# A gated mix of cached attention and an MLP on one core: the first load of wq as two transfers, 16 rows and 112 rows, and the second load of wq issued behind the end of the tile context

## The chip, the core and the metric

The kernel runs on one core of one Trainium2 chip. The metric is the device time of one execution in microseconds. Of the kernel before there are three runs: 773.12, 773.18 and 773.3 us, a median of 773.18 us. All times inside an execution come from one execution that the hardware profiler recorded, and are counted from the first instruction.

## What is computed

The reference is one decoding step for two sequences, in float32:

```python
def _A_ref(x, k_cache, v_cache, wq, wo):        # x: 2 x 1 x 1024
    q = (x @ wq)                                # 32 heads of 128
    scores = q . k_cache * Dh ** -0.5           # 4 key heads, 32768 cached positions
    o = softmax(scores) . v_cache
    return o @ wo
def _B_ref(x, w1, w2, w3, w4):
    x1 = x + hs                                 # hs: a shift by one or two positions
    return x1 + gelu(layernorm(x1) @ w3) @ w4
g = sigmoid((x * gate_w).sum(-1))
out = g * _A_ref(...) + (1 - g) * _B_ref(...)
```

With one position per sequence the shifted part `hs` is zero, so w1 and w2 are never read. What has to be read is wq (16.8 MB), w3 (14.7 MB), the caches of keys and values (268 MB together), w4 (14.7 MB) and wo (16.8 MB): 331 MB for a result of 8 KB.

## The kernel before, in words

All large arrays pass through two buffers in SBUF, `ring[0]` and `ring[1]`, each 128 rows (partitions) of 65,536 bytes. The host has laid out wq, w3, the caches, w4 and wo so that a load is 128 rows of one run of bytes each; a load of wq is a full buffer, 8 MB, and wq is two loads.

The order of the loads is written out by hand for SP (SyncE), which issues them all on its queue: wq (two loads), w3 (two), then for each of eight turns two loads of keys and two of values, w4 between the fourth and the fifth turn, and wo at the end. A load into a buffer is issued when the work on that buffer's former content is done: `load` (line 217) lets SP wait for a mark of another engine and then issues the transfer, which adds 16 to a semaphore `landed[j]` when it has landed. The engine that uses the buffer waits for that 16 and takes it off again (`take`, line 51).

The two loads of wq are the exception. They wait for nothing and are issued at line 245, inside the tile context, before it is closed (`tc.close()`, line 248, and `tc.compile()`, line 249). At the closing all engines drain their queues and meet at semaphores. Everything else in the kernel stands behind it: ScalarE issues the small load of x and the gate's weights (`xg`, line 278), GpSimd and VectorE clear buffers, and SP goes on to the loads of w3, of which the first waits for the mark `q0`.

The prologue on TensorE begins with three small products for the layernorm's sums and the padded copy of x (lines 342 to 348). Then `project` (line 361) multiplies x by wq: for each of the two loads it takes 16 off `landed[T]`, runs 64 matmuls over that buffer and sets a mark, `q0` after the first and `q1` after the second. The same function is called again for w3, with the marks `h0` and `h1`.

The rows and the engines that move them matter here: `run(wq, j)` (line 221) is the view of load j as 128 rows, and `flat[j]` (line 224) is the buffer as 128 rows. The output store at the end (line 640) takes 8 rows of a small buffer, rows 28 to 35, of 1 KB each.

Of the kernel before, what the change touches and what calls it, by code (L numbers as in the profile page):

```python
# [14 lines left out]
P = 128  # L15
B, D, HQ, HKV, SK, DH, F = 2, 1024, 32, 4, 32768, 128, 3584
# [12 lines left out]
CHUNK = D // G // 2  # L29
ROWS = G * B // 2  # L30
BASE = C - ROWS


class Line:
# [39 lines left out]
def kernel(  # L74
# [52 lines left out]
    nc = tc.nc  # L127
    scale = DH ** -0.5

    def new(name, *shape, parts=P):  # L130
        return nc.alloc_sbuf_tensor(name, [parts, *shape], F32).ap()

    def bank(name):
        return nc.alloc_psum_tensor(name, [P, 512], F32).ap()
# [6 lines left out]
    x_pad = new("x_pad", KD, C)  # L141
# [6 lines left out]
    o_last = o_wide[:, :, C - B:]  # L148
    spread = new("spread", BASE + ROWS + C)
    w_pad = new("w_pad", KF, C)  # L150
# [33 lines left out]
    sc = [bank(f"sc{i}") for i in range(NI)]  # L184
# [10 lines left out]
    def sem(name):  # L195
        cleared.append(nc.alloc_semaphore(name))
        return cleared[-1]

    stored = nc.alloc_semaphore("stored")
    pe, dve, act, pool = (Line(e, sem(n)) for e, n in (  # L200
        (nc.tensor, "pe"), (nc.vector, "dve"), (nc.scalar, "act"), (nc.gpsimd, "pool")))
    sp = Line(nc.sync)

    landed = [sem(f"landed{i}") for i in range(2)]
# [3 lines left out]
    copied = sem("copied")  # L208
    middle = slice(BASE, BASE + 2 * ROWS)

# [6 lines left out]
    def load(dst, src, sem, *marks):  # L217
        sp.after(*marks)
        nc.sync.dma_start(dst, src).then_inc(sem, 16)

    def run(src, j):
        return src[PART * j:PART * (j + 1)].rearrange("i (q w) c -> (i q) (w c)", w=PART)

    flat = [t.rearrange("p w c -> p (w c)") for t in ring]
# [7 lines left out]
    def at(name, m=None):  # L232
        if m is None:
            return (pe.sem, 1 + PROLOGUE.index(name))
        return (pe.sem, len(PROLOGUE) + m * len(TURN) + m // 4 * 2 + 1 + TURN.index(name))
# [6 lines left out]

    early = [nc.sync.dma_start(flat[j], run(wq, j)).then_inc(landed[j], 16) for j in range(2)]
    for inst in early:
        tc.no_tile_sem_insts.add(inst.ins.name)
    tc.close()
    tc.compile()

    load(flat[0][:, :PART * 2 * F], run(w3, 0), landed[0], at("q0"))
    load(flat[1][:, :PART * 2 * F], run(w3, 1), landed[1], at("q1"))

# [59 lines left out]
    dve.after(at("run"), zeroed)  # L313
    nc.vector.tensor_copy(spread[:, BASE:][:, :2 * ROWS], compact)
    for i in range(2):
        own = slice(i * HALF, (i + 1) * HALF)
# [34 lines left out]
    def columns(t, pad, k, kk, n, banks):  # L351
        quarter = n // G
        for c, b in enumerate(banks):
            lo, hi = c * 512, min(c * 512 + 512, quarter)
            for g in range(G):
                o = kk * n + g * quarter
                last = nc.tensor.matmul(b[C * g:C * g + C, :hi - lo], pad[:, k], t[:, o + lo:o + hi],  # L357
                                        start=(k == 0), stop=(k == KD - 1))
        return last

    def project(pad, n, banks):
        for T in range(4 // PART):
            pe.take(landed[T], 16)
            for kk in range(2 * PART):
                last = columns(flat[T], pad, 2 * PART * T + kk, kk, n, banks)
            done = pe.mark(last)
        return done
# [16 lines left out]
    def block(c, *quarters, **flags):  # L384

        def lhsT(half, quarter):
            return o_wide[:, c, C - B - (1 - half) * BASE - quarter % 2 * B:][:, :C]

# [8 lines left out]
                          lambda which, t: so_far[:, t * CHUNK:(t + 1) * CHUNK], (0, None), (1, None))  # L397

    pe.after(d_x)
    done = project(x_pad, HQ * DH, sc[0:2])  # L400
    dve.after(done)
    d_q = dve.mark(nc.vector.tensor_copy(row[:, 0], sc[0]))
    act.after(done)
# [14 lines left out]
    done = pe.mark(last)  # L418
    dve.after(done)
    for i in range(2):  # L420
        own = slice(i * HALF, (i + 1) * HALF)
# [9 lines left out]
    for k2 in range(2):  # L431
        for g in range(G):
            lo = P * (1 - k2)
            nc.tensor.matmul(acc[C * g:C * g + C], xr_pad[:, 2 * g + k2], wide[:, lo:lo + 2 * P],
                             start=(k2 == 0), stop=False, skip_group_check=True)
    done = project(xn_pad, F, sc[2:4])
    dve.after(done)
    d_h = dve.mark(nc.vector.tensor_copy(row[:, 0], sc[2]))
    act.after(done)
    a_h = act.mark(nc.scalar.copy(row[:, 1, :F // G - 512], sc[3][:, :F // G - 512]))  # L440
    n = KF // G
# [13 lines left out]
    done = pe.mark(last)  # L455
# [10 lines left out]
    for i in range(2):  # L466
        for j in range(2):
            own = slice(i * HALF, (i + 1) * HALF)
# [139 lines left out]
    for t, apart, lo, n in ((w_pad, C // B, 0, half), (o_last, 1, half, 2)):  # L608
        for i in range(2):
            own = slice(i * HALF, (i + 1) * HALF)  # L610
# [65 lines left out]
```

## Time and profile before

| What | Value |
|---|---|
| median of three runs | 773.18 us (773.12 to 773.3) |
| span of the profiled execution, first to last instruction | 771.6 us; a time of its own is not given beside it |
| median less span | 1.6 us |
| TensorE's matmuls busy | 436.4 us, 57% of the span |
| packets of SP's queue, as a share of 16 DMA engines | 99.4% |
| read from memory | 331.36 MB, 429 GB/s over the span |
| SP's issue of the two loads of wq | from 0.73 us, 0.87 us together |
| issue of xg, from ScalarE | 2.39 us |
| first matmul on wq | 28.38 us |
| issue of the first load of w3 | 38.09 us |

A busy share of an engine is an average over the whole span. The row of the DMA engines says how much of the time the 16 engines hold a packet; a packet here is mostly one row of a load, 65,536 bytes. A stretch of time in a view counts a packet where it starts, so a short stretch can show more than 100%.

### The profile page before, as it was taken

The page shows a single profiled execution, that of the slowest core. Times are in us where ns is not written, and L with a number is a line of the kernel's source. Part 1 is how long each engine was busy: PE and PEld are TensorE (multiplying, and loading weights), DVE is VectorE, ACT ScalarE, POOL GpSimd, SP SyncE. Part 2 cuts the span into 40 slices and gives each one's busy share as a digit, 9 for nine tenths or more (in the row PEclk, how much of TensorE's full clock was granted, in tenths as well). Part 3 has the DMA queues.
Part 4 walks back from the last instruction along what each step waited for, and adds up shares of the span by engine and source line. Part 5 has one row for each costly group of instructions (what it writes and reads, how often), then busy time and mean ns, then how long its engine had stood idle before and what let it go on. Part 6 is the DMA issues. An engine that isn't in the chain of part 4 may idle for free. (4 is left out here: it accounts for less than half of the span.)

```text
span 771.6 us, 7439 instructions
## 1 busy us (share of the span) xinstructions
PE 436.4 (57%) x3332; PEld 199.9 (26%) x3332; DVE 95.2 (12%) x269; ACT 60.7 (8%) x144; POOL 3.8 (0%) x13
## 2 busy tenths in 40 slices
PE   0676746564645474546575446454745565646467
PEld 0232413232322232223233213121322232313134
DVE  1110202100210021002100002100210021002110
ACT  0000002000200020002000002000200020002000
POOL 1000000000000000000000000000000000000000
PEclk9977667767787768767766678777777677678788
DMA  9999999999999999999999999999999999999997
GB/s 381 435 436 436 435 436 435 436 436 431 428 431 431 435 435 435 435 435 435 430 428 440 432 435 435 435 435 435 435 435 435 431 431 435 431 435 431 431 424 327
DMA packets 6648, 331.50 MB, mean 430 GB/s; under 512 B 872, under 2 KB 1008, under 8 KB 1264
## 3 DMA queue, kind: packets, MB, share of 16 engines
q1 hardware_dynamic: 6496, 331.36, 99.4%
q8 instruction: 7, 0.11, 0.1%
q10 hardware_dynamic: 144, 0.01, 0.0%
q14 instruction: 1, 0.01, 0.0%
HBM read 331.36 MB, written 0.01 MB: 429 GB/s over the span
## 5 line engine op out<-in xcount | busy, mean ns | idle before, releaser
L488 PE MATMUL sc<-load,q_cur 128*32 128x512 f32 x1024 | 144.1, 722 | 132.3 <-PEq L53 132.3
L514 PE MATMUL pv<-load,pt 128*32 128x512 f32 x1024 | 134.2, 683 | 88.7 <-PEq L53 88.7
L488 PEld LDWEIGHTS sc<-load,q_cur 128*32 128x32 f32 x1024 | 51.2, 130 | 219.2 <-issue 214.8
L514 PEld LDWEIGHTS pv<-load,pt 128*32 128x32 f32 x1024 | 39.2, 124 | 173.9 <-issue 173.9
L505 PE MATMUL sc<-wide,p 128*128 128x128 f32 x256 | 44.5, 347 | 22.8 <-PEq L53 22.8
L571 DVE TENSOR_REDUCE mx<-sc 128x1 f32<-128x512 f32 x32 | 21.4, 689 | 284.8 <-PE sc L488 284.8
L555 ACT ACT_TABLE_LOAD x8 | 10.3, 1283 | 483.0 <-ACTq L53 483.0
L505 PEld LDWEIGHTS sc<-wide,p 128*128 128x128 f32 x256 | 40.1, 184 | 30.0 <-issue 30.0
L371 PE MATMUL acc<-load,w_pad 128*32 128x256 f32 x448 | 34.2, 478 | 18.9 <-PEq L53 18.9
L588 DVE COPY pt<-sc 64x256 f32<-64x256 f32 x64 | 25.9, 414 | 81.4 <-PE sc L505 80.9
L561 ACT COPY pt<-sc 64x256 f32<-64x256 f32 x64 | 23.5, 368 | 85.3 <-PE sc L505 83.0
L593 DVE COPY pv_sb<-pv 128x512 f32<-128x512 f32 x16 | 10.3, 686 | 145.6 <-PE tr L520 145.6
L371 PEld LDWEIGHTS acc<-load,w_pad 128*32 128x32 f32 x448 | 18.6, 137 | 33.6 <-issue 28.7
L524 PE MATMUL tr<-sel,pv_sb 128*128 128x8 f32 x128 | 18.9, 284 | 11.8 <-PEq L53 11.8
L555 ACT ACTIVATE p<-sc,bias 128x512 f32<-128x512 f32 x32 | 21.6, 686 | 0.1
L357 PE MATMUL sc<-load,x_pad 128*32 128x512 f32 x128 | 19.2, 768 | 4.1 <-PEq L53 4.1
L524 PEld LDWEIGHTS tr<-sel,pv_sb 128*128 128x128 f32 x128 | 18.4, 228 | 12.3 <-issue 12.3
L357 PE MATMUL sc<-load,xn_pad 128*32 128x384 f32 (+1 forms) x128 | 15.3, 641 | 7.9 <-PEq L53 7.9
L342 PE MATMUL tr<-xg_sb,perm 128*128 128x16 f32 x4 | 1.0, 372 | 25.2 <-DMA xg_sb<-xg 25.2
L584 DVE COPY p<-p 128x256 f32<-128x256 f32 x32 | 9.4, 294 | 26.7 <-ACT p L555 26.7
L357 PEld LDWEIGHTS sc<-load,xn_pad 128*32 128x32 f32 x128 | 4.8, 130 | 18.4 <-issue 18.4
L357 PEld LDWEIGHTS sc<-load,x_pad 128*32 128x32 f32 x128 | 4.9, 137 | 17.6 <-issue 17.5
(89 smaller groups left out, 96.3 us busy)
## 6 DMA issues: line engine op xcount, KB each, us to landing
load<-w SPq DMA_DIRECT2D x4, 7168.0 KB, 24.9
load<-wo SPq DMA_DIRECT2D x1, 7168.0 KB, 29.0
load<-wo SPq DMA_DIRECT2D x1, 4608.0 KB, 19.3
load<-wo SPq DMA_DIRECT2D x1, 2560.0 KB, 25.0
tail<-wo SPq DMA_DIRECT2D x1, 1024.0 KB, 27.0
tail<-wo SPq DMA_DIRECT2D x1, 640.0 KB, 28.1
load<-kt SPq DMA_DIRECT2D x16, 29.6
load<-vt SPq DMA_DIRECT2D x16, 29.5
```

What stands on the lines that cost most here:

```text
L357: last = nc.tensor.matmul(b[C * g:C * g + C, :hi - lo], pad[:, k], t[:, o + lo:o + hi], start=(k == 0), stop=(k == KD - 1))
L371: inst = nc.tensor.matmul(acc[C * g:C * g + C], lhsT, rows[:, g * (D // G):(g + 1) * (D // G)], start=False, stop=last, skip_group_check=True)
L488: last = nc.tensor.matmul(sc[i][C * g:C * g + C], q_cur[:, w, s], ring[j][:, w, o:o + 512], start=(s == 0 and w == 0), stop=(s == 1 and w ...
L505: last = nc.tensor.transpose(sc[k][:, t * P:(t + 1) * P], pair.rearrange("p w q -> p (w q)"), ident)
L514: last = nc.tensor.matmul(pv[C * g:C * g + C], pt[j][w][:, lo:lo + C], ring[j][:, w, o:o + G * DH], start=(j == 0 and w == 0 and t == 0), ...
L524: last = nc.tensor.matmul(tr[1][:, w * REP:(w + 1) * REP], pv_sb[:, s, w].rearrange("p i q -> p (i q)"), sel[:, s], start=(s == 0), stop=( ...
L555: nc.scalar.activation(p[:, i, :, :PART], sc[i].rearrange("p (t q w) -> p t w q", t=NT, w=PART), AF.Exp, bias=bias, scale=scale, accum_out ...
L561: nc.scalar.copy(*halves(1, j, c)).then_inc(pt_in, 1)
L571: last = [nc.vector.reduce_max(out=mx[:, k:k + 1], in_=sc[k], axis=AX.X) for k in ((1, 2) if i == 2 else (i,))][-1]
L584: nc.vector.tensor_copy(p[:, i, :, PART], p[:, i, :, 0]).then_inc(to_pe, 1)
L588: nc.vector.tensor_copy(*halves(0, j, c)).then_inc(pt_in, 1)
L593: last = nc.vector.tensor_copy(pv_sb[:, :, :, i], pv.rearrange("p (s q w) -> p s w q", q=HALF, w=PART))
```

## The change

The first load of wq is cut in two at row 16. Both pieces are issued before the tile context is closed, one behind the other, and each adds 16 to the first load's semaphore when it has landed, which therefore comes to 32. `project` takes as many sixteens off the semaphore as there were transfers: two for the first half of wq, one elsewhere. The second load of wq moves from line 245 to the first place behind the closing and is issued by `load` without a mark to wait for.

```diff
+FIRST = 16
...
-    early = [nc.sync.dma_start(flat[j], run(wq, j)).then_inc(landed[j], 16) for j in range(2)]
+    early = [nc.sync.dma_start(flat[0][own], run(wq, 0)[own]).then_inc(landed[0], 16)
+             for own in (slice(0, FIRST), slice(FIRST, P))]
     for inst in early:
         tc.no_tile_sem_insts.add(inst.ins.name)
     tc.close()
     tc.compile()
 
+    load(flat[1], run(wq, 1), landed[1])
     load(flat[0][:, :PART * 2 * F], run(w3, 0), landed[0], at("q0"))
     load(flat[1][:, :PART * 2 * F], run(w3, 1), landed[1], at("q1"))
...
-    def project(pad, n, banks):
+    def project(pad, n, banks, loads=(1, 1)):
         for T in range(4 // PART):
-            pe.take(landed[T], 16)
+            pe.take(landed[T], 16 * loads[T])
...
-    done = project(x_pad, HQ * DH, sc[0:2])
+    done = project(x_pad, HQ * DH, sc[0:2], (2, 1))
```

## The prediction

> **What bounds the kernel now.** I read the page's own summary first: span, activity in 40 slices, and the DMA queues.
>
> ```profile
> span 771.6 us, 7439 instructions
> PE 436.4 (57%) x3332; PEld 199.9 (26%) x3332; DVE 95.2 (12%) x269; ACT 60.7 (8%) x144; POOL 3.8 (0%) x13
> ...
> DMA  9999999999999999999999999999999999999997
> GB/s 381 435 436 436 435 436 435 436 436 431 428 431 431 435 435 435 435 435 435 430 428 440 432 435 435 435 435 435 435 435 435 431 431 435 431 435 431 431 424 327
> ...
> q1 hardware_dynamic: 6496, 331.36, 99.4%
> ...
> PE 1%; DVE 0%; issue 0%
> ```
>
> The 16 DMA engines hold packets of SP's queue (q1) for 99.4% of the span, at a flat 435 GB/s. PE is busy 57%. The flow dips only in the first slice and the last. So the kernel is one long transfer of 331 MB, and time that an engine loses anywhere in it is hardly made up: the 0.6% in which q1 is not busy is 4.6 us, and most of it is the head and the tail. The chain of waits that ended last covers 1% of the span, its end, so it says nothing of the start, where the change lies. I went on to the DMA view of single stretches: the last line before "issues" is a queue's packets, MB and the time of its packets as a share of 16 engines in that stretch.
>
> The first packets (0 to 3 us), then the second ones (4 to 6 us):
>
> ```profile
> q1 hardware_dynamic: 16, 1.05, 106.3%
> ```
>
> ```profile
> q1 hardware_dynamic: 16, 1.05, 121.0%
> ```
>
> In each stretch 16 packets start, of 1.05 MB together, so each is one row of 65,536 bytes and each engine starts one. The second ones take 1.21 x 2 us x 16 / 16 = 2.42 us, which is 65,536 B / 2.42 us = 27.1 GB/s per engine, and 16 x 27.1 = 433 GB/s, the flat rate above. The first ones take 1.063 x 3 us = 3.19 us. I call 2.42 us a **slot**: a load of wq is 128 rows, 8 slots of each engine, 19.3 us.
>
> Then the start, from the timeline, and the finely cut table by stretches (second column: length; the last two: DMA share and GB/s), which has the first packet of wq, and below it the first packet of the output store:
>
> ```profile
> 0.73 0.87 SPq L245 DMA_DIRECT2D load<-wq  x2
> 2.39 0.42 POOL L279 MEMSET wide<- 128x384 f32 x1 [1.95 <-POOLq L249]
> 2.39 0.37 ACTq L278 DMA_DIRECT2D xg_sb<-xg  x1
> ...
> 25.10 0.17 DVE L309 TENSOR_TENSOR xw<-xg_sb 128x16 f32<-128x16 f32 x1 [18.75 <-DMA xg_sb<-xg]
> ...
> 28.38 1.94 PE L357 MATMUL sc<-load,x_pad 128*32 128x512 f32 x8
> ```
>
> ```profile
> 1.70:1.75 0.05, 0.00 (x0) 0.00 (x0) 0.00 (x0) 0.00 (x0) 0.00 (x0) 1.00 0.00 0
> 1.75:1.80 0.05, 0.00 (x0) 0.00 (x0) 0.00 (x0) 0.00 (x0) 0.00 (x0) 1.00 20.15 6554
> ```
>
> ```profile
> 38.09 0.33 SPq L219 DMA_DIRECT2D load<-w  x1
> ```
>
> ```profile
> 770.23 0.37 SPq L640 DMA_DIRECT2D out<-out_sb  x1
> ```
>
> ```profile
> 770.90:771.00 0.10, 0.00 (x0) 0.00 (x0) 0.00 (x0) 0.00 (x0) 0.00 (x0) 1.00 0.00 0
> 771.00:771.05 0.05, 0.00 (x0) 0.00 (x0) 0.00 (x0) 0.00 (x0) 0.00 (x0) 1.00 0.24 61
> ```
>
> SP issues both loads of wq from 0.73 to 1.60, and the closing of the tile context (L249) lets the engines go at 2.39. The DMA flows from 1.75 on. The first w3 load is issued at 38.09, when PE has done with the first half of wq; by the slots, both wq loads are through at 1.77 + 0.77 (the first packets' excess) + 16 x 2.42 = 41.3. Issue to first packet is 1.0 us, so some 2 us of cover remain there.
>
> **The change, part by part.**
>
> *Two issues for the first load.* SP still issues two transfers ahead of the closing (16 and 112 rows, where it was 128 and 128), at about 0.4 us each, so xg and the memsets still start at 2.39. The store has 8 rows and goes from issue 770.23 to packet about 771.02, 0.8 us; wq has 128 rows and goes from 0.73 to about 1.77, 1.04 us. If the rows make the difference, 16 rows start up to 0.24 us sooner; if not, 0. I take -0.2, as 16 is nearer to 8 rows.
>
> *The second piece* is issued 0.4 us behind the first, so its packets are due at about 2.2, while the first packets last until 1.77 + 3.19 = 4.96. No gap; were that cover gone, it would cost the 0.4 us of one issue.
>
> *The second load of wq behind the closing.* Its issue goes from 1.2 to 2.39, past the drains and semaphores of the closing in SP's queue. Its packets are needed when the first load ends, at about 21.9 us. Cover: 18 us; cost 0. Behind it on SP stands only the first w3 load, which waits for PE until 38.09 anyway.
>
> *PE's wait for 32 instead of 16* on the first landing is one instruction as before: 0. First wq lands at 21.9, PE starts on it at 28.38 (it waits for x), so 6.5 us of delay of this load alone are hidden from PE, but not from the DMA engines themselves.
>
> *Which rows are in flight together.* This is the part that decides, and no transfer of before shows it: every large one spans all 128 rows. The nearest is the output store, of 8 neighbouring rows (28 to 35); its packets, from 770.9 to 771.3 us:
>
> ```profile
> DMA packets 16, 0.01 MB, mean 21 GB/s; under 512 B 8, under 2 KB 16, under 8 KB 16
> ...
> q1 hardware_dynamic: 16, 0.01, 8.0%
> ```
>
> Eight data packets and eight small completions: eight rows went to eight engines, a row each. So 16 rows will go to 16 engines, rows 0 to 15 all at once. Before, each engine had eight of the 128 rows. Now suppose that the way into SBUF, and not the engine, is what carries 27.1 GB/s, and that a way serves eight fixed rows (128 / 16). Then 16 neighbouring rows use fewer than 16 ways. If neighbours lie on different ways, the cost is 1 slot, as now; if a way has eight adjacent rows, only 2 ways are used and the piece takes 8 slots. I take **4 slots** (four ways), the power of two just above the middle (2.8) of 1 and 8. The store speaks mildly against: 8.0% x 0.4 us x 16 = 0.51 us for 8 packets and 8 completions, at most 64 ns per KB, where a fourfold shared way would give 1,024 B / 27.1 GB/s x 4 = 151 ns. But its packets are too short to be surely in flight together, and they read SBUF, where the load writes it.
>
> For the 112 rows the same supposition works on seven consecutive rows per engine (112 / 16). Where nobody shares it is 7 slots, where each engine shares with one other all the time it is 14. I take **11**, the middle rounded up, as sevens don't fall on the borders of sets of eight.
>
> [...]
>
> *Sum.* The first load takes 4 + 11 = 15 slots of the slowest engine instead of 8: 7 x 2.42 = **+16.9 us**. It isn't made up, since every later load gives each engine its eight rows. x comes late too: its packets wait behind rows (2.39 to 25.10, 9 slots), so it comes about 7 slots later, at 42; PE is done with the first half of wq at 38.1 + 16.9 = 55.0, and the wq loads end at 41.3 + 16.9 = 58.2. The cover of 2 us there stays. Base: the profiled execution has a span of 771.6; its own time is not given beside it, so I take the median of the runs, 773.18, 1.6 above the span, and leave that distance as it is. 773.2 - 0.2 + 16.9 = **789.9 us**.
>
> **Rivals.**
>
> *No sharing* (the engine, not the way, is the limit): 1 + 7 slots as before, and only the earlier start is left: 773.2 - 0.2 = 773.0, between 772.9 and 773.2. For it: the store's short packets, and a rate that is as flat as an engine's own limit would make it. Against it: nothing in the trace singles out the engine. This is the case on the other side: not slower, and it decides as soon as a way carries four rows at full rate, 4 x 27.1 = 108 GB/s.
>
> *Only the first piece collides*: 4 slots, then 7 without sharing, or 8 if the ways that stood idle meanwhile still have eight rows to take. +3 to +4 slots: 7.3 to 9.7 us less 0.2, 780.3 to 782.7. For it: the 112 rows may be dealt to engines as the 128 are, which run clean.
>
> *The 112 rows are dealt out by every 16th*: row 16 to the first engine, 17 to the second. Then each of the seven rounds is like the first piece, 8 x 4 = 32 slots instead of 8, +58 us, 831. For it: the store gave neighbours to different engines; against it, that also fits blocks, as a block there was one row.
>
> *The pieces leave a gap*, so that the split does not do what it says: at most one issue and its latency, 0.4 + 1.0 us, if the second piece were generated only after the first is through; 774.4. The 128-row loads already follow one another without a gap, so I count it in with no sharing.
>
> **How the numbers follow.** The forecast with sharing in both pieces 0.48, only the first piece 0.18, every 16th 0.08, no sharing with or without a gap 0.26. Sharing in one form or another has 0.74: its loss is 7 to 58 us, and I have no form of it below 0.2% (1.55 us, about what a measurement of this kernel can tell from no change). Faster by over 0.2% would take 1.55 us at the head, where 0.24 is to be had: 0.01; the rest of no sharing, 0.25, is within. The forecast's own range is 785 to 797: 9 to 14 slots in the place of 11, which is 5 to 10 slots lost. The range for 8 in 10 runs from no sharing, 772.8, to 795; it leaves out every 16th and the far end of the forecast.
>
> **What would show it.** Right: 16 first packets of some 9.7 us instead of 3.19 in the first microseconds, packets of the next rows that take 2.4 to 5 us, DMA rates of 100 to 350 GB/s up to some 38 us and 435 after, x at about 42, the first w3 issue at about 55. Wrong: second packets of 2.42 us that start at 5 us and x still at 25; then the sum is the head alone. If the first packets take 9.7 and the following 2.42, the 11 was wrong; if the w3 issue comes after the wq loads have ended, a gap joins the sum that I have put at nothing.

## The result, and the profile after

The changed kernel takes **794.8 us** (median of five runs, 793.67 to 795.82), the kernel before 773.18 us beside it (773.11 to 773.3). The ratio is 1.0278, with a 95% interval of 1.0265 to 1.029: slower by 21.6 us. The profiled execution of the changed kernel took 794.8 us itself, with a span of 793.3 us, 1.5 us less; in the kernel before the distance was 1.6 us, so all of the difference lies inside the span.

The changed kernel's page, its summary, the DMA row and the rate in 40 slices (one slice is 19.8 us):

```profile
span 793.3 us, 7440 instructions
PE 433.2 (55%) x3332; PEld 199.2 (25%) x3332; DVE 95.1 (12%) x269; ACT 60.6 (8%) x144; POOL 3.8 (0%) x13
...
DMA  9999999999999999999999999999999999999997
GB/s 159 265 413 418 429 426 427 453 430 424 426 439 446 430 426 426 439 446 430 426 433 426 448 430 426 433 436 443 430 426 433 436 443 426 430 433 426 440 422 315
...
q1 hardware_dynamic: 6512, 331.36, 99.3%
```

The engines look as busy as before, 99.3% against 99.4%, and the same 331.36 MB go through. Only the rate tells: 159 and 265 GB/s in the first two slices, where it was 381 and 435, somewhat less than before in the third and fourth, and the old rate behind. The loss of the first two slices against before is (381 - 159 + 435 - 265) / 435 x 19.8 = 18 us. So a packet that crawls counts as busy, and the busy share of the DMA engines says nothing of their speed; the GB/s beside it does. The 16 more packets (888 under 512 B against 872) are the completions of the one transfer more.

The start of the changed kernel, from the timeline and from the table by stretches (last two columns: DMA share and GB/s):

```profile
0.73 0.85 SPq L246 DMA_DIRECT2D load<-wq  x2
2.36 0.35 SPq L220 DMA_DIRECT2D load<-wq  x1
2.37 0.42 POOL L282 MEMSET wide<- 128x384 f32 x1 [1.93 <-POOLq L251]
2.37 0.38 ACTq L281 DMA_DIRECT2D xg_sb<-xg  x1
...
46.98 0.18 DVE L312 TENSOR_TENSOR xw<-xg_sb 128x16 f32<-128x16 f32 x1 [40.65 <-DMA xg_sb<-xg]
...
59.30 0.35 SPq L220 DMA_DIRECT2D load<-w  x1
```

```profile
1.70:1.75 0.05, 0.00 (x0) 0.00 (x0) 0.00 (x0) 0.00 (x0) 0.00 (x0) 1.00 0.00 0
1.75:1.80 0.05, 0.00 (x0) 0.00 (x0) 0.00 (x0) 0.00 (x0) 0.00 (x0) 1.00 52.39 6554
...
12.00:22.00 10.00, 0.00 (x0) 0.00 (x0) 0.00 (x0) 0.00 (x0) 0.00 (x0) 1.00 0.80 210
22.00:32.00 10.00, 0.00 (x0) 0.00 (x0) 0.00 (x0) 0.00 (x0) 0.00 (x0) 1.00 0.93 230
32.00:42.00 10.00, 0.00 (x0) 0.00 (x0) 0.00 (x0) 0.00 (x0) 0.00 (x0) 1.00 1.09 276
42.00:52.00 10.00, 3.67 (x20) 2.28 (x24) 2.30 (x15) 1.42 (x2) 0.00 (x0) 1.00 0.93 400
```

The closing ends at 2.37 as before (2.39), and the first packet starts between 1.75 and 1.80 as before: nothing starts sooner. From 12 to 42 us the DMA moves 210 to 276 GB/s, about half of the 435 of before. x, whose small packets go between the rows (the first starts at 15.54 us, before at 7.34), comes at 46.98 instead of 25.10, 21.9 us later; PE's first mark and with it the first w3 load come 21.2 us later.

The first packets, those that start between 0 and 3 us, in the DMA view of the changed kernel:

```profile
q1 hardware_dynamic: 16, 1.05, 288.0%
```

They last 2.88 x 3 us = 8.64 us on average; before it was 3.19. Last, the loads of wq issued ahead of the closing, from issue to landing (shortest, median, longest), in the kernel before and in the changed one:

```profile
DMA to landing us min/median/max: 21.9/31.4/40.8
```

```profile
DMA to landing us min/median/max: 12.3/27.8/43.4
```

The first load of wq was issued at 0.73 and landed at 22.6. Now its 112 rows, issued at 1.2, land at 44.6: 22.0 us later. That is the whole difference of the kernel (21.6 us), and it is all in one load of 8 MB.

### The profile page after: what moved, and what is told of

It reads as the page before. It is cut to its first block, busy times and chain, and to the rows that moved or that the text cites. A ratio compares the mean times of both kernels' runs of the same rounds, so it can differ in the third digit from the quotient of the medians.

```text
span 793.3 us, 7440 instructions
## 1 busy us (share of the span) xinstructions
PE 433.2 (55%) x3332; PEld 199.2 (25%) x3332; DVE 95.1 (12%) x269; ACT 60.6 (8%) x144; POOL 3.8 (0%) x13
## 3 DMA queue, kind: packets, MB, share of 16 engines
q1 hardware_dynamic: 6512, 331.36, 99.3%
HBM read 331.36 MB, written 0.01 MB: 418 GB/s over the span
## 5 line engine op out<-in xcount | busy, mean ns | idle before, releaser
L508 PE MATMUL sc<-wide,p 128*128 128x128 f32 x256 | 44.6, 347 | 22.8 <-PEq L54 22.8
L360 PE MATMUL sc<-load,xn_pad 128*32 128x384 f32 (+1 forms) x128 | 15.1, 632 | 10.6 <-PEq L54 10.6
L360 PEld LDWEIGHTS sc<-load,xn_pad 128*32 128x32 f32 x128 | 4.8, 126 | 21.1 <-issue 21.1
## 6 DMA issues: line engine op xcount, KB each, us to landing
load<-wo SPq DMA_DIRECT2D x1, 7168.0 KB, 27.1
```

What stands on the lines that cost most here:

```text
L508: last = nc.tensor.transpose(sc[k][:, t * P:(t + 1) * P], pair.rearrange("p w q -> p (w q)"), ident)
```

## The experiments

Theory W is the prediction's supposition: fixed rows share a way into SBUF that carries as much as one DMA engine, 27.1 GB/s. A way is the supposition's word; the runs show how long chosen rows take, not which rows share a way. "Before" is always the kernel before, run beside the experiment on the same chip.

### Which part of the change costs

**Cut by columns, not by rows** (e1_columns):

```diff
-    early = [nc.sync.dma_start(flat[0][own], run(wq, 0)[own]).then_inc(landed[0], 16)
-             for own in (slice(0, FIRST), slice(FIRST, P))]
+    early = [nc.sync.dma_start(flat[0][:, own], run(wq, 0)[:, own]).then_inc(landed[0], 16)
+             for own in (slice(0, 2048), slice(2048, PART * WIDE))]
```

> As the changed kernel, but the first load of wq is cut by columns: the first 8 KB of all 128 rows, then the other 56 KB of them. Theory W (rows that are written at once share ways into SBUF): all 128 rows are in flight as before, no sharing, 773.2 us within 0.5, first packets of 8 KB well under 1 us. Theory T (two transfers for one load, with 16 more completions, are what costs): 794.8 us as the changed kernel.

Measured: 773.03 us against 773.16, ratio 0.9998 (0.9989 to 1.0008). Two transfers for one load cost nothing here, where each spans all 128 rows; theory T falls.

**The move alone** (e2_move_only):

```diff
-    early = [nc.sync.dma_start(flat[j], run(wq, j)).then_inc(landed[j], 16) for j in range(2)]
+    early = [nc.sync.dma_start(flat[0], run(wq, 0)).then_inc(landed[0], 16)]
...
+    load(flat[1], run(wq, 1), landed[1])
```

> The first load of wq in one transfer of 128 rows, the second behind the closing of the tile context. Theory W: the second load is needed only at 22 us, so 773.2 us within 0.3, with the closing over some 0.4 us sooner (1.97 instead of 2.39 us) and nothing gained by it. Theory M (the late second load opens a gap): up to 794.8 us.

Measured: 773.24 us against 773.16, ratio 1.0003 (0.9993 to 1.0012). With one issue less ahead of it the closing ends sooner:

```profile
1.92 0.38 ACTq L280 DMA_DIRECT2D xg_sb<-xg  x1
...
25.26 0.18 DVE L311 TENSOR_TENSOR xw<-xg_sb 128x16 f32<-128x16 f32 x1 [19.37 <-DMA xg_sb<-xg]
```

x is asked for 0.47 us sooner than before (2.39) and comes at 25.26, no sooner than before (25.10): its packets wait behind rows of wq (the first starts at 7.28 us here and at 7.34 before), and the sooner issue buys no place further ahead.

**The split alone** (e3_split_only): the change with the second load put back ahead of the closing.

```diff
+    early.append(nc.sync.dma_start(flat[1], run(wq, 1)).then_inc(landed[1], 16))
...
-    load(flat[1], run(wq, 1), landed[1])
```

> 16 and 112 rows, and the second load of wq right behind them, all three ahead of the closing. Theory W: 794.8 us within 1.5, as the changed kernel; the closing ends some 0.4 us later (2.8 us). Theory M: 773.2 us.

Measured: 795.41 us against 773.16, ratio 1.0286 (1.0269 to 1.0304). The split by rows is the whole cost, the move none of it.

**Two halves** (e4_halves): `FIRST = 64`.

> As the changed kernel, but cut at row 64: two transfers of 64 rows. [...] If only small first pieces collide: below 780.

Measured: 794.45 us against 773.16, ratio 1.0275 (1.0258 to 1.0292); +21.3 us. The second packets, those that start from 6 to 9 us:

```profile
q1 hardware_dynamic: 16, 1.05, 170.9%
```

1.709 x 3 us = 5.13 us for a row, for all 16 engines, where 2 slots are 4.84: 2.12 slots. Read by W as two engines on one way, that is 2 x 65,536 B in 5.13 us, 25.6 GB/s together, and not 27.1: 6% beside the halving. Large pieces collide too, here at 5.13 us a row where 128 rows take 2.42.

### Where the rows collide: written or read

Four kernels put one extra 1 MB transfer ahead of the first load of the kernel before. It fills a part of the second buffer that the second load of wq, issued when the extra has landed, writes again; so the price of that one transfer stands by itself. The edit, with the two views that differ:

```diff
+    extra = sem("extra")
-    early = [nc.sync.dma_start(flat[j], run(wq, j)).then_inc(landed[j], 16) for j in range(2)]
+    early = [nc.sync.dma_start(DST, SRC).then_inc(extra, 16),
+             nc.sync.dma_start(flat[0], run(wq, 0)).then_inc(landed[0], 16)]
...
+    load(flat[1], run(wq, 1), landed[1], (extra, 16))
```

`x1_near`: DST `flat[1][:16]`, SRC `run(wq, 1)[:16]`.

> The kernel before with one extra transfer ahead of its first load: rows 0 to 15 of the second load of wq into rows 0 to 15 of its buffer, which the whole second load writes again later (issued behind the closing, when the extra has landed). 1 MB of extra transfer and nothing else. Theory W: rows 0 to 15 reach four ways, 4 slots of 2.42 us, +9.7 us, 782.9 us. Theory E (only the engines limit): 1 slot, +2.4 us, 775.6 us. Theory D (sixteen neighbouring rows collide where they are read, not where they are written): 782.9 us too.

`x2_far`: DST `flat[1][::8]`, SRC as in x1_near.

> The same extra 1 MB, read from the same sixteen neighbouring rows in memory, but written to rows 0, 8, 16 to 120 of the buffer. [...] If a way were eight adjacent rows, they lie on sixteen ways: 775.6 us. Theory D: as the near one, 782.9 us.

`x3_near_dram_far`: DST as in x1_near, SRC `run(wq, 1)[::8]`.

> The extra 1 MB is read from every eighth row in memory and written to rows 0 to 15 of the buffer. Theory W: as the near one, 4 slots, 782.9 us. Theory D: the reads are spread, 775.6 us.

`x4_all_rows`: DST `flat[1][:, :2048]`, SRC `run(wq, 1)[:, :2048]`.

> The extra 1 MB is the first 8 KB of all 128 rows, written to the same. Every theory: all ways, 1 slot, +2.4 us, 775.6 us, perhaps 0.5 more for 128 smaller packets; it is the price of 1 MB against which the others are read.

Before, beside all four: 773.13 us.

| Extra 1 MB | us | over before | ratio, 95% interval | expected by W |
|---|---|---|---|---|
| x1_near: rows 0 to 15 from neighbouring rows | 782.49 | +9.36 | 1.0120 (1.0103 to 1.0137) | +9.7 |
| x2_far: every eighth row from neighbouring rows | 778.26 | +5.13 | 1.0066 (1.0049 to 1.0083) | no figure: W does not say which rows share |
| x3_near_dram_far: rows 0 to 15 from every eighth row | 782.33 | +9.20 | 1.0118 (1.0101 to 1.0135) | +9.7 |
| x4_all_rows: all 128 rows, 8 KB each | 775.43 | +2.30 | 1.0029 (1.0018 to 1.0041) | +2.4 |

The first packets (0 to 3 us) of x1_near, x2_far and x3_near_dram_far:

```profile
q1 hardware_dynamic: 16, 1.05, 284.2%
```

```profile
q1 hardware_dynamic: 16, 1.05, 156.8%
```

```profile
q1 hardware_dynamic: 16, 1.05, 290.0%
```

The packets last 8.53, 4.70 and 8.70 us on average. Where the rows are read makes no difference (9.36 and 9.20 us), where they are written makes a factor of nearly two (9.36 and 5.13): the collision is on the SBUF side, and theories D and E fall. The 775.6 us expected of x2_far for ways of eight adjacent rows are not met either (778.26). The 9.36 us of x1_near for 1,048,576 B are 112 GB/s, 4.1 times the 27.1 GB/s of one engine.

### What the 112 rows do

Three more kernels of the same form, with 64 or 112 rows of `run(wq, 1)` as the extra transfer, into the rows of the same numbers, and one that reads its 64 rows from the key cache instead.

`y1_64_from_32`: rows 32 to 95.

> The kernel before with an extra transfer of 64 neighbouring rows, rows 32 to 95 of the second load of wq into the same rows of its buffer, written again by that load later. [...] If 64 neighbouring rows always share two by two, as rows 0 to 63 did (2.12 slots per row): 8.5 slots, +20.5 us, 793.6 us.

Measured: 783.13 us against 773.07, ratio 1.013 (1.0113 to 1.0147), +10.06. The 64 rows of y1_64_from_32 go at the full rate; rows 0 to 63 (e4_halves) took 5.13 us per row, twice as long. The packets that start between 5.0 and 7.4 us:

```profile
q1 hardware_dynamic: 16, 1.05, 101.1%
```

1.011 x 2.4 = 2.43 us for a row, a slot.

`y2_64_from_28`: rows 28 to 91.

> The same with rows 28 to 91: one of the ways is shared by two engines all along, the other 14 engines have a way each. Theory O (sharing slows only the engines that share): 14 engines take 4 slots and two take 8 to 10, 792.5 to 797 us, and most packets last 2.42 us. Theory C (engines that share hold back the others): all 16 engines take about 2 slots for each row, packets of about 5 us throughout, 792.5 to 794 us.

Measured: 797.36 us against 773.07, ratio 1.0316 (1.0298 to 1.0333), +24.3; that is 0.4 us above theory O's range and 3.4 above C's, so the packets have to tell. The same window:

```profile
q1 hardware_dynamic: 16, 1.05, 115.0%
```

A mean of 1.15 x 2.4 = 2.76 us: 14 packets of 2.42 and two of 5.14 give that mean, and the packets' own records show it. A record has a packet's start and length, but not its engine; I join packets into a chain where one starts within some 40 ns of another's end, which gives 16 chains, and take each for an engine. In slots of 2.42 us, successive packets of single engines (four rows of the extra, then the rows of the first load of wq):

```
13 engines            1.2  1.0  1.0  1.0  | 1.2  1.25 1.25 1.25 1.25 1.1 1.0 ...
2 late engines        1.95 2.1  3.1  3.3  | 1.3  1.0  1.0 ...
1 more, slow later    1.2  1.0  1.0  1.0  | 2.9  3.3  1.45 1.0 ...
```

While two engines take 1.95 and 2.1 slots for their first two rows, the 14 others take 1.2 and 1.0: that is theory O, and C falls for this case. That two engines share a way here stood on no run before this one, and the records show it only as two slow engines beside 14 others. But the shift by four rows cost 14.2 us over y1_64_from_32. A third engine takes 2.9 and 3.3 slots for its fifth and sixth row, just while the two late ones take 3.1 and 3.3 for their last two. I read it, by W, as an engine whose rows of the next load lie on the way that the two share; the records give no rows, so this is not shown. In the same time the 13 others slow down too, to 1.25 slots.

`y3_112`: rows 16 to 127, the second piece of the change, from an even start.

> The same with rows 16 to 127, the 112 rows of the changed kernel, from an even start. Theory O, blocks of seven: the engines take 7 to 11 slots, the slowest 11, 773.1 + 26.6 = 799.7 us. Theory C: all engines take alike, and as in the changed kernel 12 to 13 slots, 802.1 to 804.5 us. No sharing at all: 7 slots, 790.0 us.

Measured: 804.14 us against 773.07, ratio 1.04 (1.0383 to 1.0417), +31.1, which is 31.07 / 2.418 = 12.85 slots for seven rows per engine. Successive packets of single engines, joined as above, in slots, here and in the changed kernel (the first packet there is one of the 16 rows):

```
y3_112, typical              1.9  1.97 1.4  1.2  1.9  1.95 1.85 | 1.5  1.0 ...
changed kernel, typical  3.5 2.2  1.97 1.25 1.57 1.85 1.95 1.82 | 1.3  1.0 ...
```

Each engine has seven rows of the 112, and all 16 show nearly the same row of figures, so O with blocks of seven is refuted here, and C's time is met.

`y4_pitch`: as y1_64_from_32, but SRC is rows of the key cache that lie 112 KB apart.

> The extra transfer writes rows 32 to 95 as before (no way shared), but reads rows that lie 112 KB apart in the key cache, so that the blocks of four rows of neighbouring engines lie 448 KB apart, as the blocks of seven do with 112 rows. Theory P (the even slowness of all engines with 112 rows comes from the distance at which they read): packets of 4 to 5 us, +17 to 20 us, 790 to 793 us. Theory W (only shared ways count): 783.1 us as with the rows read from wq, packets of 2.42 us.

Measured: 783.71 us against 773.13, ratio 1.0136 (1.0119 to 1.0153), +10.6, 0.5 more than with the same rows read from wq, where theory P expected 17 to 20. The distance at which the engines read is not why 112 rows go slowly and evenly.

## Why the prediction was right, and where it was off

**Direction and cause** were right. The step on which it hung was that rows written at once share ways and that nothing later makes it up. For its first half the runs show that it depends on the rows written how long they take: x1_near against x2_far (same reads, other rows written, +9.36 and +5.13 us) and y1_64_from_32 against e4_halves (as many rows, others, 2.43 and 5.13 us a row). Its second half is shown by the landing of the first load, 22.0 us later, beside the kernel's 21.6. That the way and not the engine is the limit could not be read from the trace of before, as the prediction said: every large transfer there spans all 128 rows, and at their flat 435 GB/s the two look alike.

**The first piece**, taken at 4 slots or 9.7 us, measured 9.36 us by itself (x1_near), 3.87 slots. The 4 was a choice between 1 and 8 for which no row of before spoke; as far as the trace goes, that it came out was luck. **The 112 rows** were the term that was mis-sized: taken at 11 slots, measured 12.85 (y3_112), 1.85 slots or 4.5 us more. The two measured prices less the 8 slots of the load that they replace give 9.36 + 31.07 - 19.34 = 21.1 us; the change cost 21.6, so the sum closes within 0.5 us. The 11 was the author's middle of 7 and 14, of an engine that shares with nobody and one that shares with one other all the time; no run shows 11 slots. By that estimate some engines are slowed more than others, and here all 16 took about as long. Why all 16 engines are slowed alike with 112 rows stays open: the reads are excluded (y4_pitch, 0.5 us), and two engines slowed by themselves did not do it (y2_64_from_28, 1.0 to 1.2 slots in the 14 others). Either the 112 rows are dealt to the engines in another way than in blocks of seven, or several shared ways hold back everyone, as the 13 others fell to 1.25 slots in y2_64_from_28 while three engines were slow; no run here tells these apart.

**The earlier start** of 0.2 us did not come: the first packet starts between 1.75 and 1.80 us with 16 rows as with 128. The 0.24 us between the store and the load, read as the price of the rows, is not that. In the records of e4_halves, y1_64_from_32 and x2_far the first packet starts only at 2.07 to 2.14 us, with 64 rows or with 16 rows eight apart; why is open, and it makes up most of the 0.4 us by which y1_64_from_32 cost more than its four slots.

**The move at nothing** was right (e2_move_only), and so was the cover by which the second piece and the third transfer leave no gap. x came at 46.98, predicted 42; the first w3 load at 59.30, predicted 55: both late by the mis-sized term. The second load of wq lands some 21.9 us later than before, at 63.9 us, with the w3 load issued at 59.30, so the 2 us of cover ahead of the w3 load stayed.

**The rivals.** No sharing, one slot for the 16 rows, is excluded by every run that writes 16 neighbouring rows (8.53 to 8.70 us for their packets). Only the first piece: by y3_112. Every sixteenth row: at the prediction's 4 slots for 16 neighbouring rows it would have taken 28 slots for the 112 rows, where y3_112 has 12.85, and e4_halves would have shown 4 slots per row, not 2.12. A gap between the pieces: by the joined packets of the changed kernel no engine waits as much as 0.1 us between its first row and its next. The store's short packets, held mildly against sharing, misled: they last 0.04 to 0.07 us and start over 0.13 us, too short and too spread to tell, and they read SBUF, which no run here tests.

## What to carry to other kernels

In a kernel that is one long stream, look at GB/s and packet lengths, not at the DMA engines' busy share: a packet that takes 8.64 us for a row counts as busy like one that takes 2.42 (99.3% here, with the first 20 us at 159 GB/s). Before cutting a load by rows, write down which rows are in flight at once and where each lands; a cut by columns (e1_columns, 773.03 us against 773.16) cost nothing here where a cut by rows cost 21.6 us. A lag of a few engines in one load was paid nearly in full at the end: in y2_64_from_28 two engines took 10.5 slots for their four rows, and the kernel took 10.05 slots (24.3 us) longer. I put that down to the later loads, which would give the slow engines as many rows as the others; no run here tests it.

## What the runs showed that was not expected

- A row takes 5.13 us in e4_halves, 2.12 slots and not 2: two engines move 25.6 GB/s together, not 27.1.
- Starting four rows earlier (28 to 91 instead of 32 to 95) cost 14.2 us more for as many rows: two engines take 10.5 slots for their four rows, and from about their fifth slot on a third engine is as slow as they are (y2_64_from_28).
- While three engines were slow (2.9 to 3.3 slots per row), the 13 others took 1.25 slots per row (y2_64_from_28).
- The runs of the changed kernel differ by 2.2 us (793.67 to 795.82), those of the kernel before by 0.2. Slow rows alone are not the reason: in e4_halves, at 2.12 slots per row, they differ by 0.14 us.
